# The per-head turn of odd heads by 64x64 quarters of the TensorE array

## The chip, the cores and the metric

The kernel runs on one core of a Trainium2 chip. Its engines are TensorE (PE, with its weight loads listed apart as PEld), VectorE (DVE), ScalarE (ACT), GpSimd (POOL) and SyncE (SP, which issues most DMAs). The metric is the device time of one execution in microseconds (us); the time before is 954.22 us, the median of 3 runs (954.05 to 954.25).

## The reference

Attention over 8 batches x 8 heads with 576 tokens of 64 channels, with a threshold under the row maximum, and after it a mixture of 8 experts of which each token takes one:

```python
scores = scale * np.matmul(q, k.transpose(0, 1, 3, 2))
thresh = np.max(scores, axis=-1, keepdims=True) - tau
scores = np.where(scores >= thresh, scores, -1000000000.0)
...
attn = attn / (np.sum(attn, axis=-1, keepdims=True) + 1e-09)
return np.matmul(attn, v).astype(np.float32)
...
logits = x @ w_gate
e_idx = np.argmax(logits, axis=1)
...
h = np.maximum(x[mask] @ w1[e], 0.0)
ye = h @ w2[e]
out[mask] = gate_w[mask, None] * eom[mask, e, None] * ye
```

All of it is float32.

## The kernel before

**Units and steps.** Two batches (a = 0, 1) of one head make a unit u; there are 32. Batch 0's head lies on partitions 0 to 63 and batch 1's on 64 to 127. The 576 tokens are 4 blocks of 128 and a rest of 64. A pass over two units (an even and an odd one) has nine steps t: 0 to 3 are the four blocks of the even unit, 4 is the rests of both, 5 to 8 the blocks of the odd unit. `run` (L347) writes the order of each engine's work out by hand; every engine runs its own list in order.

**A step.** PE multiplies queries and keys (`scores`, L143; at t = 4 by quarters of the array, L137) into two PSUM tiles `ps`. Only two such tiles exist, so the scores of the next step need DVE to have read them. DVE copies them scaled to `s` with the row minimum (L151), POOL adds tau (L156), ACT takes the exponential (`exps`, L163), DVE masks and sums (`masks`, L178; this stands one step later in DVE's list). Two steps later PE turns the result by transposes, the rest part in `remainder` (L208) and eight blocks of two halves in `blocks` (L243) into the one PSUM tile `pt`; ACT copies them to `PTa` or `PTb` (L229 and L222, L254, L248 and L250). `pt` has one buffer: the transposes of the next step wait until ACT's copy L254 has read it. PE multiplies the turned blocks with v (`av_units`, L269), spread over the steps, and ACT copies that sum to `X` (L273).

**The part that is changed.** When both halves of a unit's X are there, `x_rows` (L290) turns X back into rows of tokens and takes the router's logits in the same matmul: the stationary operand is a block of X (64 channels by the tokens), the moving one 80 columns (a 64-column identity and 16 columns of router weights, `wx`). It runs at t = 0 for the even unit and at t = 4 for the odd one; the last odd unit's stands behind the last step. A float32 matmul shows as two instructions of PE and two of PEld. Batch 0 goes to PSUM tile `pa`, batch 1 to `pr`. For an even unit, each batch has five matmuls on half the rows of the array and all its columns (64x128), the last one with the rest; the two batches run side by side as a row pair. For an odd unit, the two rests come first as two 64x64 quarters that both write `pa` (batch 1's into partitions 64 to 127), and then four row pairs follow.

**What comes behind.** The rest part of the step's transposes (L208) goes into the same two PSUM tiles. ACT copies in this order: first exponential (L163), `x_copy` of `pa` (L310), L229, second exponential, `x_copy` of `pr` (L310), for even units a short copy of batch 1's rest (L312), L229, then L254. POOL scales the rows (L322) and the logits (L331). After each eighth unit DVE sums the logits over the heads (L341, four pieces, one each at t = 5 to 8), and the router's work for these tokens is spread over later steps. The expert stage follows (`Experts.run`): PE with 128x512 matmuls (L1014 to L1016, L1036 to L1038), ACT and DVE splitting weights (L820, L823) and activations (L1019, L1020).

Of the kernel before, what the change touches and what calls it, by code (L numbers as in the profile page):

```python
# [16 lines left out]
P = 128  # L17
# [4 lines left out]
class Attention:  # L22
# [267 lines left out]
    def x_rows(self, u):  # L290
        X, pp, W, h = self.X[u % 2], self.half, self.XW, u % self.H
        ps = [pool.tile([P, 512], F32, name=name) for pool, name in ((self.ps_a, "pa"), (self.ps_r, "pr"))]
        mm = lambda out, c0, n, a: self.nc.tensor.matmul(
            out, X[pp[a], c0 : c0 + n], self.wx[pp[a], h], start=True, stop=True
        )
        last = slice(self.NB * W, self.NB * W + W)
        if u % 2:
            for a in range(2):
                mm(ps[0][pp[a], last], self.M, 64, a)
        for j in range(self.NB):  # L300
            for a in range(2):
                mm(ps[a][:, j * W : j * W + W], j * P, P, a)
        if u % 2 == 0:
            for a in range(2):
                mm(ps[a][:, last], self.M - 64 * a, P, a)
        return ps

    def x_copy(self, u, px, out, xl, a):
        nc, W = self.nc, self.XW
        nc.scalar.copy(xl[:, a::2], px[a][:, 0 : (5 - a) * W].rearrange("p (j w) -> p j w", w=W))  # L310
        if a and u % 2 == 0:
            nc.scalar.copy(xl[64:P, 8], px[1][64:P, 4 * W : 5 * W])  # L312
        if out:
            out(a)
# [919 lines left out]
```

## Time and profile before

| | before |
|---|---|
| median of 3 runs | 954.22 us |
| profiled execution, its own time | 952.78 us |
| its span in the trace | 951.1 us |
| granted TensorE clock, mean | 0.997 of full speed |
| PE busy | 933.5 us (98%) |
| DVE busy | 674.9 us (71%) |
| ACT busy | 611.7 us (64%) |
| POOL busy | 317.4 us (33%) |

The span runs from the first to the last instruction. Busy times are means over two stages of different kinds: attention until about 480 us, experts behind it. A busy PE is not PE at its peak, since the end of a matmul is modelled and the drain of one covers the start of the next.

### The profile page before, as it was taken

How to read it: one execution, taken by the hardware profiler on the slowest of the kernel's cores; microseconds unless marked ns; L12 is line 12 of the kernel's file. 1: busy time of each engine (PE TensorE's matmuls, PEld its weight loads, DVE VectorE, ACT ScalarE, POOL GpSimd, SP SyncE). 2: the span in 40 equal slices, each digit the busy share in tenths (PEclk: the TensorE clock that was granted, in tenths of full speed). 3: DMA queues.
4: the chain of work that ended last, by engine and by line, in shares of the span. 5: the costliest groups of instructions: out<-in, count | busy, mean ns of one | idle time of the engine just before them, and what ended most of it. 6: DMA issues, size and time to landing. Idle time of an engine off the chain costs nothing. (4 is left out here: it accounts for less than half of the span.)

```text
span 951.1 us, 21910 instructions
## 1 busy us (share of the span) xinstructions
PE 933.5 (98%) x8329; PEld 680.9 (72%) x8329; DVE 674.9 (71%) x1605; ACT 611.7 (64%) x1211; POOL 317.4 (33%) x568
## 2 busy tenths in 40 slices
PE   8999999999999999999999999999999999999996
PEld 4666666665666656666678887778878878878885
DVE  7899999999999999999965753435535535536621
ACT  6899898898988989889863332424424434436521
POOL 4344343456634576447626310202002002002001
PEclk9999999999999999999999999999999999999998
DMA  8972112123321233212247852526526426527301
GB/s 267 289 262 82 58 66 82 42 82 108 116 82 41 82 115 108 83 42 86 91 150 242 284 184 71 178 89 220 175 89 232 163 87 241 167 89 258 132 22 45
DMA packets 71402, 126.14 MB, mean 133 GB/s; under 512 B 8703, under 2 KB 35583, under 8 KB 71296
## 3 DMA queue, kind: packets, MB, share of 16 engines
q1 hardware_dynamic: 64656, 103.71, 34.3%
q0 software_dynamic: 6640, 21.02, 5.7%
q8 instruction: 66, 1.08, 0.5%
q14 instruction: 40, 0.33, 0.1%
HBM read 95.26 MB, written 30.22 MB: 132 GB/s over the span
## 5 line engine op out<-in xcount | busy, mean ns | idle before, releaser
L163 ACT ACTIVATE p<-s,mn 128x576 f32<-128x576 f32 x288 | 213.5, 782 | 45.3 <-DVE s L151 43.8
L178 DVE SCALAR_TENSOR_TENSOR p<-s,thr,p 128x576 f32<-128x576 f32 x288 | 231.2, 839 | 1.9 <-POOL thr L156 1.9
L151 DVE TENSOR_SCALAR_CACHE_REDUCE s<-ps 128x576 f32<-128x576 f32 x288 | 206.2, 753 | 33.2 <-PE ps L143 31.1
L1019 ACT ACTIVATE hh<-ph 128x512 fp32r<-128x512 f32 (+2 forms) x96 | 49.2, 512 | 205.1 <-PE ph L1016 199.8
L156 POOL TENSOR_SCALAR thr<-mn,tau_sb 128x2 f32<-128x2 f32 x144 | 97.5, 677 | 193.0 <-DVE s L151 190.0
L143 PE MATMUL ps<-qk 64*128 64x288 f32 x1024 | 155.9, 418 | 0.0
L1020 DVE SCALAR_TENSOR_TENSOR hl<-ph,hh 128x512 fp32r<-128x512 f32 (+2 forms) x96 | 55.5, 578 | 139.9 <-ACT hh L1019 136.5
L1014 PE MATMUL ph<-xh,w1h 128*128 128x512 f32 (+2 forms) x384 | 136.0, 354 | 0.0
L1016 PE MATMUL ph<-xh,w1l 128*128 128x512 f32 (+2 forms) x384 | 133.5, 348 | 0.2 <-issue 0.2
L1015 PE MATMUL ph<-xl,w1h 128*128 128x512 f32 (+2 forms) x384 | 133.4, 347 | 0.2 <-DVE xl L823 0.2
L1036 PE MATMUL py<-w2h,hh 128*128 128x512 f32 x304 | 120.3, 396 | 0.9 <-ACT hh L1019 0.9
L1038 PE MATMUL py<-w2h,hl 128*128 128x512 f32 x304 | 120.5, 396 | 0.6 <-DVE hl L1020 0.6
L811 POOL DMA_INDIRECT out_dram<-yo,kid x39 | 42.7, 1095 | 233.0 <-DVE yo L810 86.7
L1037 PE MATMUL py<-w2l,hh 128*128 128x512 f32 x304 | 120.0, 395 | 0.0
L269 PE MATMUL pa<-PTb,vld 128*64 128x320 f32 x640 | 101.3, 444 | 2.2 <-ACT X L273 1.5
L143 PEld LDWEIGHTS ps<-qk 64*128 64x128 f32 x1024 | 92.1, 188 | 14.5 <-DVE s L151 1.9
L243 PE MATMUL pt<-ident,p 64*128 64x64 f32 x2304 | 96.6, 223 | 3.5 <-ACT PTb L254 1.8
L243 PEld LDWEIGHTS pt<-ident,p 64*128 64x128 f32 x2304 | 83.5, 139 | 6.0 <-ACT PTb L254 4.9
L1014 PEld LDWEIGHTS ph<-xh,w1h 128*128 128x128 f32 x384 | 72.1, 188 | 11.9 <-issue 0.8
L823 DVE TENSOR_TENSOR w1l<-r,w1h 128x1024 fp32r<-128x1024 f32 x52 | 63.7, 1225 | 22.8 <-ACT w1h L820 21.9
L269 PE MATMUL pa<-PTa,vld 128*64 128x256 f32 x640 | 79.7, 387 | 0.0
L1015 PEld LDWEIGHTS ph<-xl,w1h 128*128 128x128 f32 x384 | 72.2, 188 | 10.1 <-DVE xl L823 0.6
(199 smaller groups left out, 1514.7 us busy)
## 6 DMA issues: line engine op xcount, KB each, us to landing
r<-in_moe_w_dram SPq DMA_DIRECT2D x104, 512.0 KB, 4.1
qk<-in_qkv_dram SPq DMA_DIRECT2D x31, 608.0 KB, 3.9
vld<-in_qkv_dram SPq DMA_DIRECT2D x32, 320.0 KB, 3.7
xs<-zrow SPq DMA_DIRECT2D x32, 257.0 KB, 8.2
xg<-xs SPq DMA_DIRECT2D x6, 1028.0 KB, 5.2
xg<-xs SPq DMA_DIRECT2D x4, 514.0 KB
xg<-xs SPq DMA_DIRECT2D x2, 771.0 KB
out_dram<-yo,kid POOLq DMA_INDIRECT x39
```

Source lines behind the costliest of these rows:

```text
L143: nc.tensor.matmul(ps[a][:, cs], q[pp, t * P : t * P + P], k[pp, ks(self.R * (1 - a))], start=True, stop=True)
L151: nc.vector.tensor_scalar(s, ps[a][:, c0 : c0 + S], SC, None, op0=ALU.mult, op1=ALU.min, accum_out=mn[:, a : a + 1])
L163: self.nc.scalar.activation(e, s, AF.Exp, bias=mn[:, a : a + 1], scale=-1.0)
L178: nc.vector.scalar_tensor_tensor(e, s, thr[:, a : a + 1], e, op0=ALU.is_le, op1=ALU.mult, accum_out=sums[a])
L243: nc.tensor.transpose(pt[:, o : o + 64], p[hs[h], k0 : k0 + P], id_[hs[h], hs[h]])
L269: nc.tensor.matmul(pa[self.half[a], 0:N], vm[:, kb, a], PT[:, 4 * a + kb if i else self.NK - 1], start=(i == 0), stop=(i == self.NB), skip ...
L1014: nc.tensor.matmul(ph, w1h[:, c, fs], self.xh[:, c, 0:N], start=(c == 0), stop=False)
L1015: nc.tensor.matmul(ph, w1h[:, c, fs], self.xl[:, c, 0:N], start=False, stop=False)
L1016: nc.tensor.matmul(ph, w1l[:, c, fs], self.xh[:, c, 0:N], start=False, stop=(c == 3))
L1036: nc.tensor.matmul(Y, hh[:, ts], wh, start=(f == 0), stop=False)
L1037: nc.tensor.matmul(Y, hh[:, ts], wl, start=False, stop=False)
L1038: nc.tensor.matmul(Y, hl[:, ts], wh, start=False, stop=(f == 7))
```

## The change

`x_rows` of odd units makes five groups of four matmuls, each on a 64x64 quarter of the array: both batches (a) and both 64-token halves of a block (c). The rest of each batch is read by both halves c, so that each batch's fifth group fills all 128 partitions of its own PSUM tile. Even units make the same matmuls as before. In `x_copy`, the short copy of batch 1's rest from `pr` (L312) is made for odd units too.

```diff
-        last = slice(self.NB * W, self.NB * W + W)
-        if u % 2:
+        for j in range(self.NB + 1):
+            cs = slice(j * W, j * W + W)
             for a in range(2):
-                mm(ps[0][pp[a], last], self.M, 64, a)
-        for j in range(self.NB):
-            for a in range(2):
-                mm(ps[a][:, j * W : j * W + W], j * P, P, a)
-        if u % 2 == 0:
-            for a in range(2):
-                mm(ps[a][:, last], self.M - 64 * a, P, a)
+                if u % 2:
+                    for c in range(2):
+                        mm(ps[a][pp[c], cs], min(j * P + 64 * c, self.M), 64, a)
+                else:
+                    mm(ps[a][:, cs], j * P - 64 * (a and j == self.NB), P, a)
         return ps
...
-        if a and u % 2 == 0:
+        if a:
             nc.scalar.copy(xl[64:P, 8], px[1][64:P, 4 * W : 5 * W])
```

## Rows read from the trace of the kernel before

**Rows 1.** Busy time of each engine in two stretches: the attention stage from 60 to 480 us, and the expert stage from 490 us on. The columns are the stretch, its length, then busy us and instructions of PE, PEld, DVE, ACT and POOL, the granted clock, DMA share and GB/s.
```profile
60.00:480.00 420.00, 414.62 (x5227) 266.23 (x5223) 389.25 (x1112) 379.15 (x834) 218.28 (x369) 1.00 0.26 83
490.00:951.00 461.00, 452.13 (x2412) 373.33 (x2412) 229.59 (x344) 176.59 (x267) 73.04 (x93) 0.99 0.47 157
```

**Rows 2.** PE's weight loads in order of time at an odd unit's step t = 4 (unit 3). Columns here and in the other timelines: start us, length us, engine, line, operation, output and inputs, count, and in brackets the idle time before and what ended it. The first row of L293 holds the four loads of the two rests and the first one of the row pairs.
```profile
74.16 0.47 PEld L293 LDWEIGHTS pa<-wx,X 64*64 64x64 f32 x5 [0.33 <-ACT X L273]
74.45 0.18 PEld L293 LDWEIGHTS pr<-wx,X 64*128 64x128 f32 x1
...
74.67 0.19 PEld L293 LDWEIGHTS pa<-wx,X 64*128 64x128 f32 x1
...
74.78 0.19 PEld L293 LDWEIGHTS pa<-wx,X 64*128 64x128 f32 x1
...
75.41 0.58 PEld L243 LDWEIGHTS pt<-ident,p 64*128 64x128 f32 x16
```

**Rows 3.** The same list, cut to the first loads of the quarters of L137 (one such load is 0.129 to 0.133 us long).
```profile
73.14 0.15 PEld L137 LDWEIGHTS ps<-qk 64*64 64x64 f32 x4
```

**Rows 4.** PE's matmuls in order of time: the quarters of L137 at the odd unit 1 (one matmul of it is 0.40 us long), and the first matmul behind `x_rows` at unit 3.
```profile
43.99 1.20 PE L137 MATMUL ps<-qk 64*64 64x288 f32 x16
...
75.40 0.22 PE L208 MATMUL pa<-ident,p 64*128 64x64 f32 x1
```

**Rows 5.** ACT in order of time at the odd unit 3, from the first exponential of step t = 4 to that of step t = 5.
```profile
75.18 0.78 ACT L163 ACTIVATE p<-s,mn 128x576 f32<-128x576 f32 x1 [0.15 <-DVE s L151]
75.86 0.47 ACT L310 COPY xl<-pa 128x400 f32<-128x400 f32 x1
...
77.02 0.42 ACT L310 COPY xl<-pr 128x320 f32<-128x320 f32 x1
77.32 0.23 ACT L229 COPY PTb<-pr 128x64 f32<-128x64 f32 x1
77.43 1.04 ACT L254 COPY PTb<-pt 128x1024 f32<-128x1024 f32 x1
```

**Rows 6.** ACT in order of time at the even unit 4, the same copies with L312 among them.
```profile
92.72 0.43 ACT L310 COPY xl<-pr 128x320 f32<-128x320 f32 x1
93.17 0.23 ACT L312 COPY xl<-pr 64x80 f32<-64x80 f32 x1
93.42 0.21 ACT L229 COPY PTb<-pr 128x64 f32<-128x64 f32 x1
93.53 1.02 ACT L254 COPY PTb<-pt 128x1024 f32<-128x1024 f32 x1
```

**Rows 7.** PE's weight loads in order of time: steps t = 5 to 7 behind the odd unit 3, then step t = 1 behind the even unit 4.
```profile
78.52 0.58 PEld L243 LDWEIGHTS pt<-ident,p 64*128 64x128 f32 x16 [0.28 <-ACT PTb L254]
79.01 0.79 PEld L143 LDWEIGHTS ps<-qk 64*128 64x128 f32 x8
...
82.25 0.79 PEld L143 LDWEIGHTS ps<-qk 64*128 64x128 f32 x8
...
95.20 0.58 PEld L243 LDWEIGHTS pt<-ident,p 64*128 64x128 f32 x16
```

**Rows 8.** The waits of the first 480 us, grouped: who waited <- for whom, us in total, times, the longest.
```profile
PEld pt L243 <- ACT PTb L254: 4.9, 15, 0.6
```

**Rows 9.** DVE in order of time from the odd unit's step t = 4 to step t = 8 (unit 3).
```profile
74.38 0.76 DVE L151 TENSOR_SCALAR_CACHE_REDUCE s<-ps 128x576 f32<-128x576 f32 x1
...
77.22 0.75 DVE L151 TENSOR_SCALAR_CACHE_REDUCE s<-ps 128x576 f32<-128x576 f32 x1
...
79.37 0.97 DVE L178 SCALAR_TENSOR_TENSOR p<-s,thr,p 128x576 f32<-128x576 f32 x1
...
80.30 0.76 DVE L151 TENSOR_SCALAR_CACHE_REDUCE s<-ps 128x576 f32<-128x576 f32 x1
...
83.53 0.76 DVE L151 TENSOR_SCALAR_CACHE_REDUCE s<-ps 128x576 f32<-128x576 f32 x1 [0.31 <-PE ps L143]
...
87.12 0.76 DVE L151 TENSOR_SCALAR_CACHE_REDUCE s<-ps 128x576 f32<-128x576 f32 x1 [0.54 <-PE ps L143]
```

**Rows 10.** DVE in order of time at steps t = 5 and 6 behind unit 7, the eighth of its batches.
```profile
138.59 0.54 DVE L341 TENSOR_REDUCE LX<-ltx 128x48 f32<-128x384 f32 x1
139.06 0.74 DVE L151 TENSOR_SCALAR_CACHE_REDUCE s<-ps 128x576 f32<-128x576 f32 x1
```

**Rows 11.** PE's weight loads of the scores of step t = 6 behind unit 7.
```profile
137.33 0.79 PEld L143 LDWEIGHTS ps<-qk 64*128 64x128 f32 x8
```

**Rows 12.** ACT's copy of `pa` at the odd units 13 and 21.
```profile
223.35 0.49 ACT L310 COPY xl<-pa 128x400 f32<-128x400 f32 x1 [0.16 <-PE pr L208]
...
342.02 0.49 ACT L310 COPY xl<-pa 128x400 f32<-128x400 f32 x1 [0.16 <-PE pr L208]
```

**Rows 13.** All engines in order of time at the last odd unit (31), whose `x_rows` lies among the first expert's matmuls.
```profile
483.81 0.47 PEld L293 LDWEIGHTS pa<-wx,X 64*64 64x64 f32 x5 [0.30 <-ACT X L273]
...
485.15 0.19 PEld L1016 LDWEIGHTS ph<-xh,w1l 128*128 128x128 f32 x1
...
485.33 0.49 ACT L310 COPY xl<-pa 128x400 f32<-128x400 f32 x1 [0.62 <-PE pr L293]
...
486.24 1.30 POOL L322 TENSOR_TENSOR rows<-xl,rinv 128x256 f32<-128x256 f32 x2 [4.57 <-ACT xl L310]
...
490.06 0.19 PEld L1038 LDWEIGHTS py<-w2h,hl 128*128 128x128 f32 x1 [0.80 <-DVE hl L1020]
```

## Prediction, made before the changed kernel ran

> **What bounds the kernel now.** I read the page first: PE is busy for 98% of the span, so a change that shortens PE's work looks like a sure gain. The busy time by stage comes next [rows 1]: in attention PE is at 414.6 of 420 us, but DVE is at 389.3 and ACT at 379.2, so three engines are close to full and take turns in being late; in the expert stage only PE is (452.1 of 461). Busy shares don't tell which of the three is late at the changed place, so I then read the timelines of PE, ACT and DVE around one odd unit, step by step.
>
> At step t = 4 PE makes the scores of the rests, then `x_rows`. What the next engines do with the scores goes past `x_rows`: DVE starts on the scores at 74.38 [rows 9], ACT's first exponential follows at 75.18 after an idle time of 0.15 that DVE ends, and from there ACT has no idle time until L254 ends at 77.43 + 1.04 = 78.47 [rows 5]. PE's transposes of step t = 5 start at 78.52 after 0.28 us of idle time that this L254 ends [rows 7], since `pt` has one buffer. The grouped waits show it as a habit: 15 times in the first 480 us, 4.9 us in all [rows 8], and 15 is the number of odd units inside the loop. From these transposes PE goes on without a choice: loads of the scores of t = 6 at 79.01, and DVE takes them at 80.30, 1.28 us later. One step on the same pair of rows is again 1.28 apart (82.25 and 83.53), and there DVE idled 0.31 for PE, and 0.54 at 87.12 [rows 7, 9]. So 1.28 is the lag at which PE is what DVE waits for, and at 80.30 it is; DVE's own work ended at nearly the same time (its second L178 starts at 79.37, and such instructions follow one another some 0.07 before the end of the first, which gives 80.27).
>
> So behind an odd unit's `x_rows` it is ACT's list, up to the end of L254, that sets when PE goes on; `x_rows` itself isn't in that chain.
>
> **The change part by part.**
>
> *Quarters in place of pairs, odd units.* Before, from the first load at 74.16 to the first matmul behind at 75.40: 1.24 us [rows 2, 4]. Of this the rests take 0.29 (74.16 to 74.45), and each pass of a row pair 0.11 (74.67 to 74.78), eight of them. After: ten passes of four quarters. No row shows a quarter pass of 80 columns behind another. The stream is estimated from L137: 16 matmuls of 288 columns lie in 1.20 us, one is 0.40 long, so the starts spread over 0.80 in three intervals, at most 0.27 each, and 80 of 288 columns make 0.07. The load of 64 columns is put at half of the pair pass, whose spacing is that of its loads, 0.055; after the first one it lies beside the stream. Ten passes make 0.055 + 10 x 0.07 = 0.76. Then the array goes back from quarters to pairs, which now stands inside the 0.29: two passes explain 0.055 + 0.14 = 0.19 of it, and 0.10 is left for the turn. With the next load of some 0.05, 0.91 us in place of 1.24: 0.33 less.
>
> Bounds: the cheapest is that of four quarters issued within 0.15 - 0.13 = 0.02 us of one another [rows 3], which leaves the 0.07 a pass and 0.33 less. The dearest that a row supports is that each quarter costs what an instruction of a row pair does, 0.11 / 2, so 40 x 0.055 + 0.15 = 2.35, 1.1 us more. Between them lie the transposes, 16 loads of which start within 0.58 - 0.14 = 0.44, 0.03 each [rows 2]; 40 of these and 0.15 make 1.35, 0.1 more. I take 0.33 less, since L137 is the same shape on the same quarters.
> On that bottom price the Trainium skill speaks against the change: the page "TensorE: Matmul & The Clock Gate", section "Wait — 56ns, not 53.3ns?", says that matmuls never start less than about 25 ns apart however small they are. Rows 3 show four loads of quarters within 0.02 us, which is no rule on a long run of them. By it 40 quarters would take an estimated 1.0 us, `x_rows` 1.15 with turn and load, and the sum below would be 0.25 us higher, by its tail alone.
>
> *What the saved time is worth inside the loop: nothing.* PE gets earlier to L208, L243 and the scores of t = 5. Those scores are taken by DVE at 77.22, between instructions of its own without idle time [rows 9]; and the transposes of t = 5 wait for ACT in any case, so the wait of 0.28 only grows. Where ACT itself waits for PE in front of its first copy, the gain counts: units 13 and 21, 0.16 each [rows 12]. If the quarters were dearer, ACT's own lead hides some: its copy starts at 75.86, L208's matmul ends at 75.40 + 0.22 = 75.62, so 0.24.
>
> *The copy L312 for odd units.* ACT's list gets one instruction between the copy of `pr` and L229, for 15 units in the loop and the last. The even units show the price with the same neighbours: from the start of L310 on `pr` to the start of L254 it is 0.81 with L312 (92.72 to 93.53) and 0.41 without (77.02 to 77.43), so 0.40 though the copy itself is 0.23 long. L254 is 0.02 shorter there (1.02 against 1.04), so its end comes 0.38 later [rows 5, 6]. In even units nobody feels this: L254 ends at 94.55 and PE's transposes start at 95.20 behind five units of the product with v [rows 6, 7]. Behind an odd unit only two such units stand there (`AV`), and nothing covers it. So L243 of t = 5 goes from 78.52 to 78.90, the scores of t = 6 and DVE's start on them from 80.30 to 80.68, and with DVE idling for PE behind that (0.31 and 0.54), all later steps move along. Bounds per unit: 0.40 at most; nothing, if something else is later. POOL isn't moved: its first instruction behind needs only L310.
>
> Something else is later at units 7, 15 and 23: these end a pair of batches, and DVE has a piece of the logit sums to do before the scores of t = 6. PE would allow 137.33 + 1.28 = 138.61, DVE starts at 139.06 [rows 10, 11]; 0.45 covers 0.38, and these cost nothing. In units 13 and 21 the 0.16 that PE gives back leaves 0.22. The other ten pay 0.38.
>
> *The last odd unit.* Here `x_rows` lies between 128x128 matmuls: 483.81 to 485.15, 1.34 us [rows 13], to which the turn to pairs in its midst contributes 0.10 that goes. After: 0.76 and the turn at the end as before, so 0.33 + 0.10 = 0.43 less, and here ACT waits for it (0.62 before its copy), POOL for ACT, and in the end PE's L1038 for DVE (0.80). ACT has room for L312 there. I take 0.43 less; bounds 0 and 0.5.
>
> Sum: 10 x 0.38 + 2 x 0.22 - 0.43 = 3.8 us. The profiled execution took 952.78 us, so 956.6; the median is 1.44 higher (954.22), so 958.0.
>
> **Rivals.**
>
> *A, the forecast*: the copy is exposed, the quarters are hidden, 958.0. Its own range is 955.5 to 960.2 (all 15 at 0.40 and no gain at the tail make 6.0).
>
> *B, PE's time counts after all*: faster. The place is PE between an odd unit's `x_rows` and the transposes of t = 5; the price is 0.33 for 15 units and 0.43 at the end, 5.4 us, so 948.8. It decides from the point where PE comes to L243 later than L254 ends. For it speaks PE's 98%; against it the 15 waits, whose 0.28 would have to be the time of a turn of the array and not a wait for ACT, and ACT's lack of idle time.
>
> *C, both are hidden*: ACT is ahead elsewhere and takes up its 0.38 before PE needs L254, or DVE is the later one at t = 6 more often than units 7, 15 and 23 show. Then only the tail counts: 953.8. For it speaks that DVE would have been ready only 0.03 before PE at 80.30; against it that 0.38 is far more than 0.03.
>
> *D, quarters at the price of an instruction of a row pair*: `x_rows` 1.1 longer, of which ACT's lead hides 0.24, so 0.86 + 0.38 in 15 units: 18.6 us, 972.8. Against it stand the four loads within 0.02.
>
> *E, the change doesn't do what it says*: the two halves c run one after the other, twenty passes of 0.07, `x_rows` 0.4 longer, 0.16 of it past ACT's lead. It adds 0.16 x 12 to the 4.2 of the copies and loses the tail: 960.3. L137, which has the same four quarters, speaks against it.
>
> **How the numbers follow.** A 0.65, B 0.12, C 0.15, D 0.04, E 0.04. A measurement of this kernel can tell about 0.2%, 1.9 us, from no change. Faster by more: B, 0.12. Within: C and the lowest edge of A, 0.17. Slower by more: the rest, 0.71. The range takes in A's own, C and the edge of E, 953.5 to 960.3; B and D are left out.
>
> **What would show it.** In the profile of the changed kernel, ACT should show L312 32 times with 0.40 from the copy of `pr` to L254 added at odd units, PE's wait for L254 before L243 of t = 5 should be up to 0.28 + 0.33 + 0.38 = 1.0 in place of 0.28 in most odd units, DVE's idle time for PE at t = 6 should go from nothing to some 0.38, and `x_rows` of odd units should shrink to about 0.9. The prediction is wrong if the transposes of t = 5 aren't released by L254 or if the interval from one odd unit's `x_rows` to the next one's doesn't grow by about 0.38 where nothing else is late.

## The result and the profile after

| | us, median | ratio to the kernel before, 95% interval |
|---|---|---|
| the change, first comparison (6 runs each) | 959.55; before 954.24 | 1.0054 [1.0042, 1.0067] |
| the change again, beside the last experiments | 957.68; before 953.54 | 1.0047 [1.0033, 1.0061] |

The change is slower by 5.3 and 4.1 us; 958.0 was predicted, 3.8 above the median of before. The profiled execution of the change took 960.1 us with a span of 958.3.

PE's weight loads of the change at unit 3, the first and last loads of `x_rows`, what follows up to the scores of t = 6, and the first load of the next `x_rows` (unit 4):

```profile
75.01 0.14 PEld L293 LDWEIGHTS pa<-wx,X 64*64 64x64 f32 x2 [0.33 <-ACT X L273]
75.03 0.14 PEld L293 LDWEIGHTS pr<-wx,X 64*64 64x64 f32 x2
...
75.63 0.14 PEld L293 LDWEIGHTS pr<-wx,X 64*64 64x64 f32 x2
75.86 0.13 PEld L208 LDWEIGHTS pa<-ident,p 64*128 64x128 f32 x1
...
75.93 0.57 PEld L243 LDWEIGHTS pt<-ident,p 64*128 64x128 f32 x16
76.42 1.09 PEld L143 LDWEIGHTS ps<-qk 64*128 64x128 f32 x8
77.89 0.63 PEld L269 LDWEIGHTS pa<-PTa,vld 128*64 128x64 f32 x8 [0.39 <-issue]
...
79.73 0.58 PEld L243 LDWEIGHTS pt<-ident,p 64*128 64x128 f32 x16 [0.69 <-ACT PTb L254]
...
91.18 0.18 PEld L293 LDWEIGHTS pa<-wx,X 64*128 64x128 f32 x1 [0.38 <-ACT X L273]
```

The same places in the kernel before, as far as they don't stand in [rows 2, 7]:

```profile
75.90 0.80 PEld L143 LDWEIGHTS ps<-qk 64*128 64x128 f32 x8
77.08 0.63 PEld L269 LDWEIGHTS pa<-PTa,vld 128*64 128x64 f32 x8 [0.39 <-issue]
...
89.97 0.18 PEld L293 LDWEIGHTS pa<-wx,X 64*128 64x128 f32 x1 [0.38 <-ACT X L273]
```

`x_rows` is shorter: from the first load at 75.01 to the first matmul of L208 at 75.87 it is 0.86 us for 1.24 [rows 2, 4]. From it to the next even unit's `x_rows` it takes longer all the same: 91.18 - 75.01 = 16.17 for 89.97 - 74.16 = 15.81, 0.36 more. In between, PE's wait for L254 has grown from 0.28 [rows 7] to 0.69.

ACT of the change at the same place:

```profile
77.87 0.42 ACT L308 COPY xl<-pr 128x320 f32<-128x320 f32 x1
78.31 0.22 ACT L310 COPY xl<-pr 64x80 f32<-64x80 f32 x1
78.56 0.21 ACT L229 COPY PTb<-pr 128x64 f32<-128x64 f32 x1
78.67 1.02 ACT L254 COPY PTb<-pt 128x1024 f32<-128x1024 f32 x1
```

From the copy of `pr` to L254 it is 0.80 for 0.41 [rows 5]. (Lines from `x_copy` on have numbers lower by 2.) DVE's first scores of t = 6 now stand behind an idle time that PE ends, where there was none [rows 9]:

```profile
81.51 0.76 DVE L151 TENSOR_SCALAR_CACHE_REDUCE s<-ps 128x576 f32<-128x576 f32 x1 [0.32 <-PE ps L143]
```

The grouped waits of the first 480 us, who waited <- for whom, us in total, times, longest, for the same pair as in [rows 8], where it was 4.9 us:

```profile
PEld pt L243 <- ACT PTb L254: 10.6, 15, 0.8
```

And the busy times, columns as in [rows 1]: first the change from 60 to 480 us, then the same work in both kernels, from the first `x_rows` to the last, before and after:

```profile
60.00:480.00 420.00, 410.38 (x5452) 262.45 (x5451) 389.54 (x1110) 379.55 (x838) 217.41 (x361) 1.00 0.26 84
31.63:483.81 452.18, 446.47 (x5606) 286.01 (x5604) 417.34 (x1187) 407.85 (x892) 230.14 (x387) 1.00 0.31 98
32.12:489.04 456.92, 445.90 (x5906) 284.70 (x5904) 418.78 (x1187) 412.12 (x907) 231.29 (x387) 1.00 0.31 97
```

From 60 to 480 us PE's busy time fell from 414.6 to 410.4 us, but these 420 us hold less of the slower kernel's work. Over the same work it is 445.9 us for 446.5, so hardly anything of the shorter `x_rows` is left in it, and PE's idle time grew from 5.7 to 11.0 us while the loop became 4.7 us longer.

### The profile page after: what moved, and what is told of

It is laid out like the page before. It is cut to its first block, busy times and chain, and to the rows that moved or that the text cites. A ratio compares the mean times of both kernels' runs of the same rounds, so it can differ in the third digit from the quotient of the medians.

```text
span 958.3 us, 22551 instructions
## 1 busy us (share of the span) xinstructions
PE 934.2 (97%) x8649; PEld 680.7 (71%) x8649; DVE 676.7 (71%) x1605; ACT 615.9 (64%) x1227; POOL 319.7 (33%) x568
## 5 line engine op out<-in xcount | busy, mean ns | idle before, releaser
L1017 ACT ACTIVATE hh<-ph 128x512 fp32r<-128x512 f32 (+2 forms) x96 | 49.1, 511 | 206.9 <-PE ph L1014 201.8
L156 POOL TENSOR_SCALAR thr<-mn,tau_sb 128x2 f32<-128x2 f32 x144 | 99.1, 688 | 196.8 <-DVE s L151 194.7
L143 PE MATMUL ps<-qk 64*128 64x288 f32 x1024 | 159.9, 419 | 0.0
L809 POOL DMA_INDIRECT out_dram<-yo,kid x39 | 44.7, 1145 | 231.5 <-DVE yo L808 84.8
L143 PEld LDWEIGHTS ps<-qk 64*128 64x128 f32 x1024 | 95.7, 189 | 15.1 <-DVE s L151 2.2
L821 DVE TENSOR_TENSOR w1l<-r,w1h 128x1024 fp32r<-128x1024 f32 x52 | 63.7, 1225 | 23.1 <-ACT w1h L818 22.3
```

Source lines behind the costliest of these rows:

```text
L143: nc.tensor.matmul(ps[a][:, cs], q[pp, t * P : t * P + P], k[pp, ks(self.R * (1 - a))], start=True, stop=True)
```

## Experiments

Differences are to the kernel before, run on the same chip beside each. "Interval" is the time from the first load of one `x_rows` to that of the next; a clean odd unit is one whose next steps hold none of the router's extra work (units 1, 3, 5 and others). Line numbers are those of each run's own kernel.

**The copy alone.** The kernel before, with the change's short ACT copy at odd units, into a tenth block of `xl` that nobody reads.

```diff
+        if a and u % 2:
+            nc.scalar.copy(xl[64:P, 9], px[1][64:P, 3 * W : 4 * W])
```

> The kernel before with nothing but one more ACT copy for odd units, of the form, the place and the PSUM tile of the change's copy, into a place that nobody reads. Theory 1: 0.38 us for 12 of the 15 units in the loop (units 7, 15 and 23 are covered by DVE, and units 13 and 21 get nothing back from PE here), 4.6 us, and no gain at the last unit: 958.8; PE's wait for L254 in front of the transposes of step 5 should be some 0.66 in place of 0.28. Rival 2: 954.2.

Measured: 958.01 us, ratio 1.0050 [1.0036, 1.0064], 4.7 us more. PE's loads at unit 3, to the next unit's first:

```profile
75.92 0.14 PEld L293 LDWEIGHTS pa<-wx,X 64*64 64x64 f32 x2 [0.33 <-ACT X L273]
...
80.64 0.58 PEld L243 LDWEIGHTS pt<-ident,p 64*128 64x128 f32 x16 [0.65 <-ACT PTb L254]
...
92.08 0.18 PEld L293 LDWEIGHTS pa<-wx,X 64*128 64x128 f32 x1 [0.38 <-ACT X L273]
```

92.08 - 75.92 = 16.16, as in the change, with the row pairs of before. At this unit the copy alone makes the whole loss. From the first `x_rows` to the last it makes 4.25 us (456.43 for 452.18), where the first profile of the change has 4.74.

**Quarters alone.** The change without that copy; at odd units the rows and logits of batch 1's last 64 tokens are left out.

```diff
-        if a:
+        if a and u % 2 == 0:
             nc.scalar.copy(xl[64:P, 8], px[1][64:P, 4 * W : 5 * W])
```

> The change without the extra copy: the rows and logits of the last 64 tokens of batch 1 are left out for odd heads (those of batch 0 stand in their place), all else is done. Quarters alone, nothing added on any other engine. Theory 1 (PE's saved time is hidden behind ACT's L254, the copy is all the loop's loss): from an odd unit's x_rows to the next even unit's as before (15.81 at clean units), units 13 and 21 0.2 longer by the 0.53 us hole in PE's transposes that the change shows there, and -0.4 to 0 from the last unit: 0 +- 0.6 us against the kernel before. Rival B (PE's time counts): 0.33 less per odd unit, 5 us less. A rival by which quarters themselves cost: 2 us more or above.

Measured: 953.86 us, 1.0004 [0.9995, 1.0013], and 3.8 us under the change, which ran beside it. Unit 3:

```profile
75.38 0.14 PEld L293 LDWEIGHTS pa<-wx,X 64*64 64x64 f32 x2 [0.33 <-ACT X L273]
...
76.79 1.08 PEld L143 LDWEIGHTS ps<-qk 64*128 64x128 f32 x8
78.26 0.63 PEld L269 LDWEIGHTS pa<-PTa,vld 128*64 128x64 f32 x8 [0.39 <-issue]
...
79.73 0.58 PEld L243 LDWEIGHTS pt<-ident,p 64*128 64x128 f32 x16 [0.32 <-ACT PTb L254]
...
91.17 0.18 PEld L293 LDWEIGHTS pa<-wx,X 64*128 64x128 f32 x1 [0.38 <-ACT X L273]
```

DVE's reading of the second PSUM tile of t = 4, first in this kernel, then in the kernel before:

```profile
76.28 0.75 DVE L151 TENSOR_SCALAR_CACHE_REDUCE s<-ps 128x576 f32<-128x576 f32 x1
```
```profile
75.06 0.76 DVE L151 TENSOR_SCALAR_CACHE_REDUCE s<-ps 128x576 f32<-128x576 f32 x1
```

The interval is 15.79, as before. PE's time here is worth nothing, and the rows show where it goes: the scores of t = 5 start 1.41 behind the first load of `x_rows` (1.74 before), but their eight loads take 1.08 for 0.80, since the second PSUM tile isn't free sooner: DVE reads it until 77.03, behind the start of these loads at 76.79, and in the kernel before until 75.82, ahead of their start at 75.90. The product with v starts at 2.88 for 2.92: 0.33 gained have become 0.04 before PE even gets to the wait for L254. The rows left out change what the router sees, but not the times: the loop is 452.12 us for 452.18, and from unit 31's first load to the end it is 467.16 for 467.25.

**Quarters, the rest taken by a wider copy.** The ACT copy of `pr` takes its fifth block along, and POOL scales the rest with two small instructions of its own.

```diff
-        nc.scalar.copy(xl[:, a::2], px[a][:, 0 : (5 - a) * W].rearrange("p (j w) -> p j w", w=W))
+        n = 5 if u % 2 else 5 - a
+        nc.scalar.copy(xl[:, a : a + 2 * n - 1 : 2], px[a][:, 0 : n * W].rearrange("p (j w) -> p j w", w=W))
...
+            nc.gpsimd.tensor_tensor(
+                R[64:P, 8, hs], xl[64:P, 9, 0:D], r[64:P, 8:9].broadcast_to([64, D]), op=ALU.mult
+            )
```

> Quarters for odd units as in the change, but without ACT's extra copy: the copy of pr takes a fifth block (400 columns in place of 320) and GpSimd scales that rest in two small instructions of its own. Theory 1 (the extra copy on ACT is exposed in odd units, the quarters are hidden): the 400-column copy of pa is 0.05 us longer than the 320-column one of pr, so L254 ends 0.05 later in place of 0.38; 10 x 0.05 less some 0.4 at the last odd unit: 954.3, no change against before. Rival 2 (the quarters themselves, or what they shift in the expert stage, make the loss): 958 to 960 as in the change. Rival 3 (PE's shorter part counts once the copy is gone): 0.33 x 15 + 0.43 = 5.4 less, 949.

Measured: 957.52 us, 1.0047 [1.0034, 1.0061], a miss. At clean units the interval grew by only 0.06, as expected, but at unit 7 by 0.35 and at units 13, 21 and 29 by 0.66, 0.93 and 0.81. Behind unit 7, POOL's added scaling and its logits, and then DVE's first piece of the logit sums:

```profile
138.68 0.69 POOL L325 TENSOR_TENSOR rows<-xl,rinv 64x64 f32<-64x64 f32 x1
139.44 0.86 POOL L334 TENSOR_TENSOR ltx<-xl,rinv 128x144 f32<-128x144 f32 x1
```
```profile
140.34 0.55 DVE L348 TENSOR_REDUCE LX<-ltx 128x48 f32<-128x384 f32 x1 [0.34 <-POOL ltx L334]
```

POOL, busy for a third of the span in the kernel before, was late for DVE's sums of logits, which stand ahead of the scores in DVE's list. At units 13, 21 and 29, where POOL also has the router's work, DVE's masks waited 1.42, 1.70 and 1.95 us for POOL's L156 (before 0.48, 0.47 and 0.99). These waits in the first 480 us, grouped, were 1.9, 3, 1.0 before and are now:

```profile
DVE p L178 <- POOL thr L156: 5.6, 5, 2.0
```

So a good part of the cost had moved to another engine.

**The copy on DVE.** The change, with odd units' copy made by DVE at once.

```diff
-            nc.scalar.copy(xl[64:P, 8], px[1][64:P, 4 * W : 5 * W])
+            (nc.vector.tensor_copy if u % 2 else nc.scalar.copy)(xl[64:P, 8], px[1][64:P, 4 * W : 5 * W])
```

> The change, but the extra copy of odd units is made by DVE in place of ACT. Theory 1 (the loop's loss is the 0.40 that the copy costs in ACT's list ahead of L254): ACT's list is as before, PE's transposes of t = 5 come at their old time; the copy costs DVE some 0.15 to 0.2 (80 of the 576 elements that take 0.68, and a start), of which PE's lead at t = 6 hides 0.03 and DVE's idle time at t = 7 (0.31) up to all: 0 to 2 us above the kernel before. Rival (the quarters or what they do to the order on PE cost the time): as the change, 4 to 5 us above the kernel before.

Measured: 1016.94 us, 1.0679 [1.0641, 1.0717]: 63.7 us more, a miss by far. DVE and then PE at unit 3:

```profile
81.31 0.24 DVE L310 COPY xl<-pr 64x80 f32<-64x80 f32 x1 [1.65 <-ACT xl L308]
81.58 1.00 DVE L178 SCALAR_TENSOR_TENSOR p<-s,thr,p 128x576 f32<-128x576 f32 x1
```
```profile
83.91 0.13 PEld L208 LDWEIGHTS pr<-ident,p 64*128 64x128 f32 x1 [2.40 <-issue]
```

ACT's next instruction, and a stretch behind PE's wait, columns as in [rows 1]:

```profile
81.58 0.21 ACT L229 COPY PTb<-pr 128x64 f32<-128x64 f32 x1 [0.31 <-DVE xl L310]
```
```profile
86.00:89.00 3.00, 3.00 (x12) 1.38 (x12) 3.00 (x11) 2.71 (x6) 0.83 (x2) 0.50 0.03 0
```

The copy waits 1.65 us for ACT's copy of the first four blocks of `pr`; behind it in DVE's list stand the masks that PE's next transposes need. The intervals behind odd units grow by 2.5 to 5.6 us. Not all of this is the wait: behind PE's wait of 2.40 us the granted clock is 0.50 from 86 to 89 us, the lower of its two levels (1.2 of 2.4 GHz). The three intervals with a granted clock of 1.00 (units 1, 5 and 9) are 2.5 longer; those in which it fell are 3.2 to 5.6 longer. Fifteen times 2.52 make an estimate of 38 of the loop's 61.6 us, and the rest goes with the lower clock.

**The copy on DVE, later.** As above, but behind DVE's masks of t = 4; POOL's scaling of that half follows it.

```diff
+            if xu is not None and xu % 2:
+                self.x_rest(px, xl)
+                self.x_out(xu, xl, (0,))
```

> The change, but the extra copy of odd units is made by DVE, behind its masks of step t = 4, where ACT's copy of pa, which writes the same cells first, has long ended; POOL's scaling of that half comes behind it. Theory 1: ACT's list is as before; the copy takes DVE some 0.16 (0.09 for 80 of 576 elements at 0.68, and a start of 0.07), which puts its scores of t = 6 at 0.13 behind PE's and which its 0.31 of idle time at t = 7 takes up in part; units 7, 15 and 23 pay it in full (0.5 in all), units 13 and 21 0.2 each for the hole: 0.5 to 2.9 us above the kernel before. Rival (the copy costs the same on any engine, or POOL's later scaling does): 4 us or more.

Measured: 960.74 us, 1.0077 [1.0063, 1.0090], 7.2 us more: the rival's side. ACT's list is indeed as before, and PE's wait for L254 is 0.32. But DVE pays, here at unit 3:

```profile
78.72 0.24 DVE L316 COPY xl<-pr 64x80 f32<-64x80 f32 x1 [0.28 <-ACT PTb L229]
79.00 0.76 DVE L151 TENSOR_SCALAR_CACHE_REDUCE s<-ps 128x576 f32<-128x576 f32 x1
```

It waits 0.28 for ACT's copies of other columns of `pr` and takes 0.28 to the next start, so the scores of t = 5 come 0.64 later (3.70 behind the first load of `x_rows`, 3.06 before); the clean interval is 0.39 longer, and units 7, 15 and 23, where DVE is the late one, pay 0.42 to 0.50.

**The copy at even units.** The kernel before with one more such ACT copy at even units, read by nobody.

```diff
+        if a and u % 2 == 0:
+            nc.scalar.copy(xl[64:P, 9], px[1][64:P, 3 * W : 4 * W])
```

> The kernel before with the same extra ACT copy for even units instead (a second one beside the one they have), into a place that nobody reads. Theory 1: PE reaches the transposes of step 1 about 0.65 us after L254 has ended there, which covers 0.38: no change, 954.2. Rival 4 (ACT's total load sets the time, wherever the copy stands): 0.38 x 16 = 6 us more, 960.3.

Measured: 954.92 us, 1.0018 [1.0009, 1.0027], 1.6 us more; nothing was expected. The interval behind even units is 0.04 longer at clean units and some 0.11 at those with the router's extra work. The copy is cheaper here, 0.12, right behind another like it:

```profile
94.42 0.22 ACT L312 COPY xl<-pr 64x80 f32<-64x80 f32 x1
94.54 0.22 ACT L314 COPY xl<-pr 64x80 f32<-64x80 f32 x1
```

A reader for L254 was there that I hadn't looked at: the product with v at t = 2 already waits 0.28 for it in the kernel before (the row at 97.34 below), and here it waits 0.39, so even units have no slack on ACT either:

```profile
98.70 0.74 PEld L269 LDWEIGHTS pa<-PTb,vld 128*64 128x64 f32 x8 [0.39 <-ACT PTb L254]
```

**Quarters at even units.** Even units' `x_rows` by quarters, where the copy stands in any case.

```diff
-                    mm(ps[a][:, cs], j * P, P, a)
+                    for c in range(2):
+                        mm(ps[a][pp[c], cs], min(j * P + 64 * c, self.M), 64, a)
```

> Quarters for the even units alone, odd units as before; the even units have their copy of the rest already. Theory 1: behind an even unit PE and not ACT is the late one, so the 0.33 us that the quarters save counts there, less what the scores of step 1 wait for DVE (their PSUM tiles come free about 0.15 us into the gain): 0.15 to 0.33 for 15 units, 2.3 to 5 us less, 949.2 to 952. Rival 5 (PE's part of these rows is hidden at even units too): 954.2.

Measured: 953.89 us, 1.0007 [0.9998, 1.0016]; a gain was expected and the time shows none. PE's loads at unit 4, first of the kernel before (its `x_rows` starts at 89.97), then of this one:

```profile
91.65 0.80 PEld L143 LDWEIGHTS ps<-qk 64*128 64x128 f32 x8
92.83 1.93 PEld L269 LDWEIGHTS pa<-PTa,vld 128*64 128x64 f32 x20 [0.38 <-ACT p L163]
...
97.34 0.26 PEld L269 LDWEIGHTS pa<-PTb,vld 128*64 128x64 f32 x4 [0.28 <-ACT PTb L254]
```
```profile
90.28 0.14 PEld L293 LDWEIGHTS pa<-wx,X 64*64 64x64 f32 x2 [0.38 <-ACT X L273]
...
91.68 0.98 PEld L143 LDWEIGHTS ps<-qk 64*128 64x128 f32 x8
93.05 1.92 PEld L269 LDWEIGHTS pa<-PTa,vld 128*64 128x64 f32 x20 [0.39 <-issue]
...
97.64 0.47 PEld L269 LDWEIGHTS pa<-PTb,vld 128*64 128x64 f32 x6 [0.35 <-ACT PTb L254]
```

From the first load of `x_rows`: scores at 1.40 for 1.68, the product with v at 2.77 for 2.86, and that of t = 2 at 7.36 for 7.37. First DVE (the tile of the scores), then ACT (L254) take the 0.28 back. The intervals aren't quite the same: behind units 2, 4, 6 and 26 they are 0.08 shorter, behind 14, 22 and 28 0.08, 0.19 and 0.22 longer; from the first `x_rows` to the last it is 452.14 us for 452.18.

**The last unit.** First the change with row pairs and no copy at unit 31, then the kernel before with quarters and the copy at unit 31 only (the diff is that of the change, under `u == self.nu - 1`).

> The change, but the last odd unit (31) makes its rows by row pairs and without the extra copy, as before. The profile of the change has ten clean odd units 0.36 longer and units 13 and 21 about 0.57 longer, 4.7 us. Theory 1 (the last unit's gain of 0.43 is taken by a wait for POOL's chain of indirect DMAs, which ends 50.9 us after x_rows of unit 31 starts in either kernel): the time is that of the change within 0.3, some 4.7 us above the kernel before. Theory 2 (the forecast's tail term stands): 0.43 above the change, 5.2 above the kernel before or more. Theory 3 (quarters at the last unit bring the long wait near 540 and the lower granted clock in it): 1.5 below the change.

> The kernel before, but the last odd unit (31) makes its rows by quarters, with the extra copy. Theory 1: no difference, 0 +- 0.2 us against the kernel before; from the start of x_rows to ACT's first instruction behind the long wait some 50.9 us, as before. Theory 2 (the forecast's tail term): 0.43 us less. Theory 3: 1.5 to 2 us more, with a granted clock under 1 near 540.

Measured: 958.86 us, 1.0060 [1.0047, 1.0073], 5.6 us more; and 952.57 us, 0.9992 [0.9983, 1.0001], 0.7 us less, with an interval from 1.6 less to 0.1 more. Both the forecast's 0.43 and no difference at all lie within it; a loss of more than 0.1 us doesn't, so theory 3 is out. It doesn't settle theory 1 against theory 2. The time from unit 31's first load to the end of the span varies too much for 0.4 us: with row pairs there 467.24 to 468.03 in six profiles, with quarters in seven 466.90 (the second kernel here) to 469.30 (the change's first); the medians are 467.25 and 467.42.

**Two controls.** The kernel before with the tile `xl` ten blocks wide and the tenth unused, and the change once more.

```diff
-                xl = self.w2.tile([P, 9, self.XW], F32, name="xl")
+                xl = self.w2.tile([P, 10, self.XW], F32, name="xl")
```

> The kernel before, with the tile xl ten blocks wide in place of nine and nothing in the tenth: a control for the three runs that copied into such a tile. Theory 1: no difference, 0 +- 0.3 us, from one x_rows to the next as before. Rival: the other addresses cost by themselves, as the first x_rows of those three runs came 0.5 to 1.2 us later than in the kernel before: 0.5 to 1.2 us more, all of it ahead of the first x_rows.

Measured: 953.27 us, 1.0000 [0.9992, 1.0009]; the first `x_rows` starts at 31.79. So the tile's width costs nothing in the experiments above.

> The change itself, beside the two runs above and the kernel before on one chip. By the intervals of its profile (ten odd units 0.36, units 13 and 21 0.57, unit 25 0.36 in place of one of them, the last unit 0 to -0.4): 4.3 to 5.1 us above the kernel before. If the 5.3 of the first comparison holds with no wait at a low clock near 540 in this profile, that wait isn't part of the change's cost.

Measured: 957.68 us, as in the table on top, 4.1 us more, just under the expected 4.3. In the first profile of the change PE waited 1.6 us for ACT's L1017 near 540 us, and the granted clock fell; in this one it waited 1.5 and the clock stayed. The stretch 540.5 to 543.5, columns as in [rows 1], first of the first profile and then of this one:

```profile
540.50:543.50 3.00, 3.00 (x8) 2.24 (x9) 2.48 (x9) 2.18 (x3) 0.00 (x0) 0.57 0.90 267
```
```profile
540.50:543.50 3.00, 3.00 (x17) 2.77 (x16) 2.86 (x10) 1.05 (x2) 0.00 (x0) 1.00 0.90 297
```

8 matmuls in place of 17 in those 3 us: from 541 to 544 us the granted clock was 0.50, the lower of its two levels (1.2 of 2.4 GHz), about 1.5 us of that profile. Without this fall the change still costs 4.1 us. The mean granted clock is 0.996 or 0.997 in four of the six runs of the first comparison and in one of the five here, so such falls may be why the first median is 1.9 us higher; no run tests that.

## Why the prediction was right, and where it wasn't

*Right.* The sign, the place and the size: 958.0 lies between 957.68 and 959.55. **The copy L312 in odd units** was put at 0.38 a unit and measures 0.36, in nine units (1, 3, 5, 9, 11, 17, 19, 25, 27). **Units 7, 15 and 23 cost nothing** held: the intervals are 16.22, 16.23 and 16.22 in the second profile of the change for 16.23, 16.16 and 16.23. DVE at unit 7 is later than PE still: scores loaded at 139.26, taken at 140.62, 1.36 behind and not 1.28, right after the piece of logit sums.

```profile
139.26 0.79 PEld L143 LDWEIGHTS ps<-qk 64*128 64x128 f32 x8
```
```profile
140.15 0.54 DVE L339 TENSOR_REDUCE LX<-ltx 128x48 f32<-128x384 f32 x1
140.62 0.74 DVE L151 TENSOR_SCALAR_CACHE_REDUCE s<-ps 128x576 f32<-128x576 f32 x1
```

**Quarters in place of pairs**: 0.86 us for a forecast of 0.91. Nine passes of four take 75.63 - 75.03 = 0.60, 0.07 each, as estimated from L137, and the turn to pairs is there: 0.23 from the last quarter's loads to L208's. That settles rivals D and E. The Trainium skill's page "TensorE: Matmul & The Clock Gate", section "Wait — 56ns, not 53.3ns?", has matmuls start at least about 25 ns apart; here 40 of them on four quarters start within 0.69 us, 0.018 each, so for quarters the trace disagrees and the price drawn from it doesn't come.

**The saved time is worth nothing inside the loop** held: quarters alone measured +0.3 us with an interval of -0.5 to +1.2, where rival B asked for -5. Rival C, that the copy is hidden, fell with the copy alone at +4.7.

*Partly luck.* That the total fits so well: the loop lost 0.4 us more than the forecast's 4.2, the 0.43 taken off for the tail isn't shown by any run, and the two medians of the change lie 1.9 us apart. Of rival A's range only the upper end is worked out; 955.5 has no sum behind it.

*Wrong in size.*

- "The wait of 0.28 only grows", to 1.0: it is 0.69, and the copy alone makes it 0.65, the quarters alone 0.32. The quarters' 0.33 is gone two groups earlier, in the scores of t = 5, whose second PSUM tile DVE hasn't read. The conclusion stood, but the cover is double: both DVE's reading of `ps` and ACT's L254 hide PE's time, and quarters at even units, where I looked for a gain, ran into the same two.
- Units 13 and 21 were put at 0.22, because PE would give back 0.16 there. They cost 0.53 and 0.56 (second profile; 0.60 and 0.55 in the first). The copy alone costs 0.37 and 0.35 there and the quarters alone 0.14 and 0.16: what was forecast as given back comes on top. PE's loads of the change at unit 13:

```profile
224.55 0.39 PEld L243 LDWEIGHTS pt<-ident,p 64*128 64x128 f32 x9
225.46 0.32 PEld L243 LDWEIGHTS pt<-ident,p 64*128 64x128 f32 x7 [0.53 <-issue]
```

  A hole of half a microsecond in the midst of sixteen equal transposes, in which PE waits for nothing that the profile shows. It is there, 0.46 to 0.56 long, at units 13 and 21 in all seven profiles with quarters at the odd units of the loop, behind units 14, 22 and 28 where even units have quarters, and in none of the kernel before, of the copy alone or of the other experiments. So it comes with the quarters. Why it stands at these units wasn't tried; quarters double PE's instructions in `x_rows` (40 matmuls for 20), and whether that has to do with it is open. The list of DMA transfers around both holes of the first profile (224.6 to 226.0 and 344.6 to 345.6 us) has none of the instruction queues.
- The tail: 0.43 less. The experiment on the last unit allows it (-1.6 to +0.1), the profiles can't show it. It stays open.
- "In even units nobody feels this": one more copy there costs 0.04 to 0.11 in most units, through the product with v at t = 2, which waits for L254 too.
- Unit 29 was counted at 0.38 and has 0.20; the interval ahead of it grew by 0.17 instead.

The sum by the second profile: 9 x 0.36 + 0.53 + 0.56 + 0.20 + 0.17 = 4.7, with small differences either way elsewhere 4.6 in the loop (456.75 us from the first `x_rows` to the last, 452.18 before), against 4.2 in the forecast.

## What to carry to other kernels

Where three engines are full and take turns at being late, look for who releases the step behind the changed one, and price a change by what it adds to that engine's list, not by what it saves on the busiest one: here 0.38 us off PE's work was worth nothing, and an ACT copy of 0.22 us cost 0.36 in most units. Moving such a copy to another engine is no way out unless that engine has slack at that very place, and a wait in the midst of an in-order list costs all that stands behind it. If the rests could be laid out so that no engine copies them apart, quarters would come out even with the pairs, and no better, as long as DVE's reading of `ps` and L254 set the pace.

## What the runs showed of the hardware

- Four 64x64 quarters with 80 columns each cost 0.07 us a pass, 64-column loads included; a row pair of the same columns costs 0.11 [rows 2]. The turn back costs: 0.23 us from the last quarter's load to the first load of a pair.
- A half-partition ACT copy of 0.22 us costs 0.39 in line between two copies of other shape (24 ns idle on either side, and no overlap with its neighbours), and 0.12 behind another like it.
- DVE's copy of columns 320 to 400 of `pr` waited 0.28 us for ACT's copy L229 of other columns of the same tile (the copy on DVE, later), and ACT's L229 waited 0.31 us for DVE's copy (the copy on DVE), though both only read `pr` and write different tiles. (The wait of 1.65 us is for a copy that also writes the same tile `xl`, so by itself it tells less.) The Trainium skill's page "PSUM — Partial Sum Buffer", section "PSUM bank collisions raise a hardware error", says that the compiler puts any two instructions of different engines that touch the same bank and 32 partitions in an order, reads too; the traces agree.
- Up to the first `x_rows` no kernel here differs, and yet it started at 31.6 to 33.0 us over the profiles: 1.4 us of spread that belongs to no change.
